# Operand sums moved to VectorE in halves, score masks moved to ScalarE and GpSimd: one fused retention and gated-unit kernel

## The chip, the cores and the metric

The kernel runs on one core of a Trainium2 chip. TensorE does the matrix products into PSUM; VectorE (DVE in the profile) and ScalarE (ACT) can read PSUM and SBUF; GpSimd (POOL) works here on SBUF only; SyncE (SP) issues most of the transfers. Each engine runs its own queue in order and waits for the others by semaphores. The metric is the device time of one execution in microseconds (us), lower is better.

## The reference, cut to what matters

```python
scores = (1/sqrt(64)) * q @ k.T                     # batch 8, heads 8, sequence 576, head dim 64
Dmat   = where(i >= j, gamma_h ** (i - j), 0)       # causal, one decay per head
x      = (scores * Dmat) @ v                        # -> 4608 tokens x 512
h      = x @ w_in                                   # 512 -> 2048
out    = (h * cos(h)) @ w_out                       # 2048 -> 512
```

The decay is a product of a power for the row and one for the column, so the kernel folds it into q and k; of `Dmat` only the 0/1 causal mask is left to be applied to the scores. Only scores inside a group of 128 tokens are formed; what earlier tokens contribute comes through a carried state per head.

## The kernel before, in words

The 4608 tokens are 36 groups of 128 (`g`). Nine groups hold two sequences of 576; the fifth of the nine (`g % PER == MIX`: groups 4, 13, 22, 31) holds the end of one sequence and the start of the next, so its mask also cuts off one more 64x64 corner per head (`tri_mix`).

Work on a group, in this order:

- `load`: three transfers (`fq`, `fk`, `fv`) on SP's queue, in rings of five buffers.
- `prep` (lines 140 and 156): GpSimd multiplies q and k by their powers into `qks` and casts v into `vb`; beyond group 25 ScalarE does the cast. `transposes` then puts a transposing transfer on SP's queue.
- `scores` (lines 195 and 207): TensorE writes the 8 heads' 128x128 scores of a group into one PSUM tile (tag "a" or "b"), VectorE multiplies them by the mask into `ret` (bf16, in SBUF; four buffers).
- `states`: TensorE forms k·v of a group, VectorE adds it to the running state (`s32`, lines 285 and 287), ScalarE casts it.
- `attn_out` (lines 319 and 333): for a pair of groups, TensorE multiplies `ret` by v (`own`, line 333) and then the carried state by q (line 319); ScalarE evacuates the result as `xT` (line 350).

The dense part goes in ten tiles of tokens, `widths = [512, 256, 256] + [512] * 7`. `mm1` (line 365) makes eight blocks of h per 512 tokens, each a PSUM tile of 128x1024 from the three tags a, b and m in turn; ScalarE computes the cosine (`cosh`, line 373), VectorE the product `gT` (line 374). A block can only start when the `gT` of the block three before it has read its PSUM tile.

Tiles n = 0, 1, 2 multiply `gT` by `w_out` directly (`mm2`). From n = 3 (`S7`) on, `mm2_seven` does the second product as a 2x2 block product in seven products instead of eight. `gT` is split in two halves r of the tokens and two halves k of the 2048 features. Each of the seven products is 16 matmuls of 256 columns (line 517) over eight features blocks. They run in the order 3, 4, 5, 2, 1, 7, 6. Products 3 and 4 take quarters of `gT` as they are; the others take a sum or difference of two quarters, a tile `gs` of 8 x 256 per partition:

```python
5: ((0, 0), (0, 1), ALU.add),      # (r, k) of the first quarter, of the second, operation
2: ((1, 0), (1, 1), ALU.add),
1: ((0, 0), (1, 1), ALU.add),
7: ((0, 1), (1, 1), ALU.subtract),
6: ((1, 0), (0, 0), ALU.subtract),
```

`g_sum` (line 445) makes them: the fifth, and a few others in tiles 3 and 9, on VectorE in pieces of 128x1024 or more, all the rest on GpSimd in pieces of 128x512, four for one sum. A hand-made dependency ("port free") holds the first GpSimd piece after a VectorE piece until that one is done. Results are combined in SBUF tiles `ot` (lines 537 and 559 on VectorE, 557, 564 and 569 on ScalarE) and stored.

Between the seven products the attention of the next tile's groups is placed (`at`, with `unit7`): two units in a tile, each with `states`, `attn_out` of one pair and `scores2` of the next pair. For n = 5 and later these stand ahead of product 4 and ahead of product 1. In tiles 3 and 4 `scores2` alone stands ahead of product 5, and units stand ahead of products 1 and 6. The order on every engine is the program's order (`manual_schedule`); nothing reorders it. After each of the four stores of a tile `feed` appends the next `prep`, transposes and loads: none after the first store, one group after the second, one after the third and two after the fourth.

Of the kernel before, what the change touches and what calls it, by code (L numbers as in the profile page):

```python
# [13 lines left out]
ALU = mybir.AluOpType  # L14
# [3 lines left out]
def kernel(  # L18
# [16 lines left out]
    nc = tc.nc  # L35
    P = 128
    B, H, S, D = q.shape
# [7 lines left out]
    PER = 2 * S // P  # L45
    MIX = PER // 2
    HP = P // 2
# [8 lines left out]
    N_PE_T = 6  # L56
    S7 = 3
    LD = 5

    consts = ctx.enter_context(tc.tile_pool(name="consts", bufs=1))  # L60
    first = ctx.enter_context(tc.tile_pool(name="first", bufs=1))
# [38 lines left out]
    tiles = {}  # L100
# [86 lines left out]
    def scores(g, bank, idle=0, parts=1, put_off=None):  # L187
        qks, vb, qkT, qT = tiles["a", g]
        ps = psum.tile([P, 2, HG, P], F32, tag=bank, name="sc")
        warm(ps[:, 0].rearrange("p b i -> p (b i)"), idle)  # L190
        for hg in range(HG):
            for i0 in range(0, P, P // parts):
                for he in range(2):
                    d0, i1 = he * D, i0 + P // parts
                    nc.tensor.matmul(  # L195
                        ps[i0:i1, he, hg, :],
                        lhsT=qkT[d0 : d0 + D, HG + hg, i0:i1],
                        rhs=qT[d0 : d0 + D, hg, :],
                        start=True,
                        stop=True,  # L200
                    )
        ret = retp.tile([P, 2, HG, P], BF16, tag="ret", name="ret")
        mask = tri_mix if g % PER == MIX else tri
        tiles["ret", g] = ret

        def masked():
            nc.vector.tensor_tensor(  # L207
                out=ret.rearrange("p a b i -> p (a b) i"),
                in0=ps.rearrange("p a b i -> p (a b) i"),
                in1=mask.unsqueeze(1).to_broadcast([P, H, P]),  # L210
                op=ALU.mult,
            )

        if put_off is None:
            masked()
        else:
            put_off.append(masked)
# [207 lines left out]
    def g_sum(n, x, e0, e1):  # L425

        gT = tiles["g", n]
        a, b, op_ = {
            5: ((0, 0), (0, 1), ALU.add),
# [4 lines that stand above are left out]
        }[x]  # L434
        if ("gs", n, x) not in tiles:
            tiles["gs", n, x] = sump.tile([P, E2, 256], BF16, tag=f"gs{x}", name=f"gs{x}")
        on_dve = x == 5 or (n, x) == (S7, 2) or (n, x, e0) in (
            (S7, 1, 4), (last, 1, 0), (last, 2, 4)
        )
        step = e1 - e0 if on_dve else 2  # L440
        for e in range(e0, e1, step):
            i0, i1 = (
                gT[:, k * E2 + e : k * E2 + e + step, r * 256 : (r + 1) * 256] for r, k in (a, b)
            )
            i = (nc.vector if on_dve else nc.gpsimd).tensor_tensor(  # L445
                out=tiles["gs", n, x][:, e : e + step], in0=i0, in1=i1, op=op_
            )
            if on_dve:
                tiles["gate"] = i
            elif "gate" in tiles:  # L450
                tc.add_manual_dep(
                    i.ins,
                    tiles.pop("gate").ins.name,
                    mybir.DependencyInfo(mybir.DependencyClass.Sync, mybir.DependencyReason.DATA),
                    reason="port free",
                )

    def sums_after(n, i):

        if n == S7:  # L460
            if i < 4:
                w_sums(3 + i % 2, i // 2 * 4, i // 2 * 4 + 4)
            elif i < 6:
                g_sum(n, 5, i % 4 * 4, i % 4 * 4 + 4)
                if i == 5:
                    g_sum(n, 6, 0, 4)
            elif i == 7:
                g_sum(n, 2, 0, E2)
                g_sum(n, 1, 4, E2)
                g_sum(n, 1, 0, 4)  # L470
                for e in (0, 4):
                    g_sum(n, 7, e, e + 4)
                prep_next(kv_first=True)
                g_sum(n, 6, 4, E2)
        elif n == S7 + 1 and i in (3, 7):
            for x in (5, 2, 1):
                g_sum(n, x, i - 3, i + 1)
            for x in (7, 6) if i == 7 else ():
                for e in (0, 4):
                    g_sum(n, x, e, e + 4)  # L480
        elif i == 3:
            for x in (5, 2, 1, 7, 6) if n < last else (5, 1, 2, 7, 6):
                g_sum(n, x, 0, 4)
        elif i == 7 and n == last:
            late_sums(n)

    def late_sums(n):
        for x in (5, 2, 1, 7, 6):
            g_sum(n, x, 4, E2)

    def product(n, x):

# [34 lines left out]
    def mm2_seven(n, at):  # L527
# [4 lines left out]
        def flush():  # L532
            while pend:
                pend.pop(0)()
# [14 lines left out]
        for x in (3, 4, 5, 2, 1, 7, 6):  # L549
            if x in at:  # L550
                at[x](flush, pend)
            else:
                flush()
            parts = product(n, x)
            if x == 3:
                u22 = new("a")
# [37 lines left out]
    def prep_next(**kw):  # L594
        nonlocal prepared
        prep(prepared, **kw)
        prepared += 1
# [182 lines left out]
    for n, w in enumerate(widths):  # L780
# [28 lines left out]
        if n == 0:  # L809
            todo = [  # L810
                (34 + 5 * i, lambda x=x, e=e: w_sums(x, e, e + 4))
                for i, (x, e) in enumerate((x, e) for x in (1, 6, 7) for e in (0, 4))
            ] + [
                (45, lambda: transposes(4, "ab")),
                (49, lambda: state(4)),
                (50, lambda: scores(4, "a")),
                (57, lambda: attn_out([4], "a")),
                (61, lambda: transposes(5, "ba")),
                (63, lambda: state(5)),
            ]  # L820
        elif n == 1:
            todo = pair(6, "ab", 16, 27)
        elif n == 2:
            todo = [(11, lambda: scores2(g)), (25, lambda: unit(g, "m", soon=True))]
            late += [lambda: unit(g + 2, "b", False)]
        else:
            at = {}
            if n + 1 < len(widths):
                at = {
                    4: lambda then, off: unit7(g, "st", True, lambda: late_sums(n), off),  # L830
                    1: lambda then, off: unit7(g + 2, "n", True, then),
                }
                if n in (3, 4):
                    at = {
                        5: lambda then, off: (then(), scores2(g)),
                        1: lambda then, off: unit7(g, "n", True, then),
                        6: lambda then, off: unit7(g + 2, "b", n > 3, then),
                    }
            mm2_seven(n, at)
            continue  # L840
# [43 lines left out]
```

## Time and profile before

| What | Value |
|---|---|
| Device time, three runs | 301.53 us median (300.94 to 304.33) |
| Profiled execution, first to last instruction | 298.2 us |
| TensorE | 287.1 us busy, 3113 matmuls |
| VectorE | 207.9 us busy, 245 instructions |
| ScalarE | 135.9 us busy, 167 instructions |
| GpSimd | 209.4 us busy, 214 instructions |
| `gs` sums on GpSimd, 128x512 | 102, together 116.3 us |
| `gs` sums on VectorE | 18, together 20.4 us |
| score masks on VectorE, 128x1024 | 36, together 43.0 us |
| `gT` on VectorE, 128x1024 | 72, together 87.8 us |
| Granted TensorE clock | 1.000 of full speed |

The profile gives the span of one execution; around it lie the 3.3 us by which the median of the runs is longer. Busy time counts from an instruction's start to its end, waits for a port of the memory inside it included; a time in brackets behind an instruction is idle time before it, with what ended it. Start times are from the beginning of the span. Tile 3's `mm1` starts at 84.18 us, those of tiles 4 to 9 at 116.78, 149.83, 179.84, 209.19, 238.62 and 267.81.

### The profile page before, as it was taken

Reading aid. Unit: us, or ns where it says so; the run is one execution under the profiler, and the core shown is the slowest. Engines: PE = TensorE matmul, PEld = TensorE weight load, DVE = VectorE, ACT = ScalarE, POOL = GpSimd, SP = SyncE. Lnnn points to the kernel's source line nnn. Section 1 sums busy time; section 2 is a strip of 40 time slices with the busy share of each in tenths; the row PEclk is TensorE's granted clock in tenths of the full one; section 3 lists DMA queues with packets and bytes.
Section 4 is the critical chain, followed back from the end, with each engine's and each line's share of the span. In section 5 each row is a group of like instructions: output and inputs, shape, how many; then the busy total and the mean of one; then the engine's idle time right before and its main releaser. Section 6 shows DMA issues by size and latency. Waiting matters only on the chain.

```text
span 298.2 us, 7384 instructions
## 1 busy us (share of the span) xinstructions
PE 287.1 (96%) x3113; PEld 195.3 (65%) x3113; DVE 207.9 (70%) x245; ACT 135.9 (46%) x167; POOL 209.4 (70%) x214
## 2 busy tenths in 40 slices
PE   8899999999999999979999999999999999999995
PEld 3478646848578786448744875488448845874584
DVE  5677637564579994788848874887489757935872
ACT  2656433514255432642346554546464446425620
POOL 2750066436445599997999999599959946980693
PEclk9999999999999999999999999999999999999999
DMA  7999999999999999999999997998690260031013
GB/s 203 212 209 206 209 214 213 200 243 208 208 174 222 211 239 213 217 279 176 198 224 229 209 200 183 212 208 201 122 194 2 73 143 0 2 106 36 0 44 99
DMA packets 154304, 50.28 MB, mean 169 GB/s; under 512 B 140832, under 2 KB 153248, under 8 KB 154272
## 3 DMA queue, kind: packets, MB, share of 16 engines
q1 hardware_dynamic: 149504, 45.10, 77.2%
q0 software_dynamic: 4224, 4.19, 8.5%
q8 instruction: 24, 0.39, 0.6%
q10 hardware_dynamic: 544, 0.52, 0.5%
q14 instruction: 8, 0.07, 0.1%
HBM read 36.70 MB, written 9.44 MB: 155 GB/s over the span
## 4 chain that ended last, share of the span: by engine, by line
PE 43%; POOL 25%; SPq 13%; DMA 8%; DVE 5%; issue 3%; ACT 1%; POOLq 0%; DVEq 0%
PE h L365 22%; POOL gs L445 17%; PE o L517 11%; SPq L117 8%; POOL qks L140 6%; PE o L382 5%; SPq L167 4%; DVE gT L374 3%; DMA fk<-in_k_dram 2%; DMA w_in_sb<-in_moe_w_in_dram 2%; DMA qkT<-qks 2%; POOL vb L156 2%; DVE gs L445 2%; DMA fv<-in_v_dram 1%; ACT cosh L373 1%
## 5 line engine op out<-in xcount | busy, mean ns | idle before, releaser
L445 POOL TENSOR_TENSOR gs<-gT 128x512 bf16<-128x512 bf16 x102 | 116.3, 1180 | 29.4 <-DVE gs L445 29.4
L365 PE MATMUL h<-xT,w_in_sb 128*128 128x512 bf16 (+2 forms) x832 | 127.6, 313 | 2.6 <-DVE gT L374 1.8
L374 DVE TENSOR_TENSOR gT<-h,cosh 128x1024 bf16<-128x1024 f32 x72 | 87.8, 1223 | 43.7 <-ACT cosh L373 40.7
L373 ACT ACTIVATE cosh<-h,half_pi 128x1024 f32<-128x1024 f32 x72 | 80.2, 1114 | 72.2 <-PE h L365 69.8
L365 PEld LDWEIGHTS <-w_in_sb 128*128 128x128 bf16 x832 | 75.9, 98 | 51.6 <-issue 3.0
L140 POOL TENSOR_TENSOR qks<-fq,gq 128x512 bf16<-128x512 f32 x32 | 34.0, 1062 | 40.9 <-DMA fq<-in_q_dram 40.9
L517 PEld LDWEIGHTS <-gs 128*128 128x128 bf16 x576 | 53.6, 98 | 10.1 <-POOL gs L445 2.9
L140 POOL TENSOR_TENSOR qks<-fk,gk 128x512 bf16<-128x512 f32 x35 | 37.3, 1066 | 8.0 <-DMA fk<-in_k_dram 7.4
L207 DVE TENSOR_TENSOR ret<-sc,tri 128x1024 bf16<-128x1024 f32 x32 | 38.1, 1217 | 2.8 <-PE sc L195 2.7
L517 PE MATMUL o<-ws,gs 128*128 128x256 bf16 (+1 forms) x352 | 39.1, 268 | 0.7 <-POOL gs L445 0.5
L382 PE MATMUL o<-w_out_sb,gT 128*128 128x512 bf16 x128 | 30.1, 380 | 0.0
L517 PE MATMUL o<-w_out_sb,gT 128*128 128x256 bf16 x224 | 26.6, 273 | 0.1
L517 PE MATMUL o<-w_out_sb,gs 128*128 128x256 bf16 x224 | 26.1, 273 | 0.5 <-POOL gs L445 0.4
L537 DVE TENSOR_TENSOR ot<-o,ot 128x512 f32<-128x512 f32 (+2 forms) x25 | 14.9, 603 | 14.7 <-PE o L517 14.5
L517 PEld LDWEIGHTS <-gT 128*128 128x128 bf16 x224 | 21.4, 98 | 4.7 <-DVE gT L374 0.7
L350 ACT CAST xT<-ov 128x1024 bf16<-128x1024 f32 (+1 forms) x18 | 16.5, 917 | 16.1 <-PE ov L319 13.9
L445 DVE TENSOR_TENSOR gs<-gT 128x1024 bf16<-128x1024 bf16 (+1 forms) x18 | 20.4, 1148 | 0.3
L382 PEld LDWEIGHTS <-gT 128*128 128x128 bf16 x128 | 11.8, 98 | 12.5
L156 POOL CAST vb<-fv 128x512 bf16<-128x512 f32 x22 | 14.3, 651 | 4.4 <-DMA fv<-in_v_dram 4.2
L564 ACT COPY ot<-o 128x512 f32<-128x512 f32 x7 | 4.1, 586 | 20.5 <-PE o L517 20.5
L392 ACT COPY ot<-o 128x512 f32<-128x512 f32 x8 | 4.7, 588 | 17.4 <-PE o L382 17.4
L537 DVE TENSOR_TENSOR ot<-ot,o 128x512 f32<-128x512 f32 x14 | 9.6, 684 | 4.0 <-ACT ot L569 2.4
(70 smaller groups left out, 175.8 us busy)
## 6 DMA issues: line engine op xcount, KB each, us to landing
out_dram<-ot SPq DMA_DIRECT2D x35, 256.0 KB, 4.0
fk<-in_k_dram SPq DMA_DIRECT2D x32, 256.0 KB, 5.2
fv<-in_v_dram SPq DMA_DIRECT2D x32, 256.0 KB, 5.2
fq<-in_q_dram SPq DMA_DIRECT2D x30, 256.0 KB, 4.5
w_in_sb<-in_moe_w_in_dram POOLq DMA_DIRECT2D x4, 512.0 KB, 8.9
w_out_sb<-in_moe_w_out_dram POOLq DMA_DIRECT2D x4, 512.0 KB, 16.2
fq<-in_q_dram SPq DMA_DIRECT2D x8, 128.0 KB, 4.0
fk<-in_k_dram SPq DMA_DIRECT2D x8, 128.0 KB, 4.4
```

The lines of the kernel that those rows point to most:

```text
L117: i = nc.sync.dma_start(f[p0:p1], src[b, :, s0 : s0 + p1 - p0, :].rearrange("h s d -> s h d"))
L140: eng.tensor_tensor(out=qks[:, m].rearrange("p (b a) d -> p a b d", a=2), in0=f.rearrange("p (a b) d -> p a b d", a=2), in1=by[:, c, :].re ...
L156: copy_v(vb, fv)
L207: nc.vector.tensor_tensor(out=ret.rearrange("p a b i -> p (a b) i"), in0=ps.rearrange("p a b i -> p (a b) i"), in1=mask.unsqueeze(1).to_br ...
L350: evac(tiles["x", n][:, :, t0 : t0 + len(gs) * P], ps.rearrange("p c x i -> p c (x i)"))
L365: nc.tensor.matmul(ps[:, j, :], lhsT=w_in_sb[:, dg, (et + j) * P : (et + j + 1) * P], rhs=xT[:, dg, c0 : c0 + w], start=(dg == 0), stop=(d ...
L373: nc.scalar.activation(cosh, ps, ACTF.Sin, bias=half_pi, scale=1.0)
L374: nc.vector.tensor_mul(gT[:, et : et + m, c0 : c0 + w], ps, cosh)
L382: nc.tensor.matmul(ps, lhsT=gT[:, et, tsi * P : (tsi + 1) * P], rhs=w_out_sb[:, et, :], start=(et == 0), stop=(et == ET - 1),)
L445: i = (nc.vector if on_dve else nc.gpsimd).tensor_tensor(out=tiles["gs", n, x][:, e : e + step], in0=i0, in1=i1, op=op_)
L517: nc.tensor.matmul(dst[i], lhsT=lhs[:, e, j * P : (j + 1) * P], rhs=rhs[:, e, c0:c1], start=(x in (3, 4, 1, 7) and e == 0 and (i == 0 or l ...
L537: pend.append(lambda: nc.vector.tensor_tensor(out=out_, in0=in0, in1=in1, op=op_))
```

## The change

All `gs` sums of tiles 3 to 9 go to VectorE, in halves of 128x1024 (ten for one tile, 70 in all), and the hand-made dependency goes. Their places in VectorE's queue are new: `sums_after` puts the first halves of sums 5, 2 and 1 behind `mm1` blocks 3, 4 and 5, `sums_before` puts the others ahead of the products, behind what `flush` or the unit has queued. In tile 3 the places differ: sums 5 and the first half of 6 within `mm1`, the second half of 6 ahead of product 4, sums 2, 1 and 7 ahead of products 5, 2 and 1.

From group 16 (`SEL`) on, 20 groups in all, the mask on VectorE is replaced by two steps: ScalarE copies the scores from PSUM into `ret`, and GpSimd sets the masked part of `ret` to zero in place (for groups 22 and 31 with a further `memset` of the corner). The copies stand in ScalarE's queue behind the `xT` evacuation of their unit and ahead of the casts of the state. `put_off` has no effect there any more.

The program order of TensorE and the order of SP's transfers are the same in both kernels.

```diff
+    SEL = 16
...
-        if put_off is None:
+        if g >= SEL:
+            nc.scalar.copy(ret.rearrange("p a b i -> p (a b) i"), ps.rearrange("p a b i -> p (a b) i"))
+            ret8 = ret.rearrange("p a b i -> p (a b) i")
+            nc.gpsimd.affine_select(
+                ret8, ret8, pattern=[[0, H], [1, P]], compare_op=ALU.is_ge, fill=0.0, base=0,
+                channel_multiplier=-1,
+            )
+            if g % PER == MIX:
+                nc.gpsimd.memset(ret8[:HP, :, HP:], 0.0)
+        elif put_off is None:
             masked()
...
-        on_dve = x == 5 or (n, x) == (S7, 2) or (n, x, e0) in (
-            (S7, 1, 4), (last, 1, 0), (last, 2, 4)
-        )
-        step = e1 - e0 if on_dve else 2
-        for e in range(e0, e1, step):
...
-            i = (nc.vector if on_dve else nc.gpsimd).tensor_tensor(
-                out=tiles["gs", n, x][:, e : e + step], in0=i0, in1=i1, op=op_
-            )
...
+        nc.vector.tensor_tensor(out=tiles["gs", n, x][:, e0:e1], in0=i0, in1=i1, op=op_)
+
+    def g_halves(n, *which):
+
+        for x, half in which:
+            g_sum(n, x, 4 * half, 4 * half + 4)
 
     def sums_after(n, i):
 
         if n == S7:
             if i < 4:
                 w_sums(3 + i % 2, i // 2 * 4, i // 2 * 4 + 4)
...
+            g_halves(n, *{4: [(5, 0)], 5: [(5, 1)], 6: [(6, 0)]}.get(i, ()))
+        else:
+            g_halves(n, *{3: [(5, 0)], 4: [(2, 0)], 5: [(1, 0)]}.get(i, ()))
+
+    def sums_before(n, x):
+
+        if n == S7:
+            todo = {4: [(6, 1)], 5: [(2, 0), (2, 1)], 2: [(1, 0), (1, 1)], 1: [(7, 0), (7, 1)]}
+        else:
+            todo = {5: [(1, 1)], 2: [(7, 0), (7, 1)], 1: [(6, 0), (6, 1)]}
+            if n < last and n != S7 + 1:
+                todo[5].insert(0, (2, 1))
+            else:
+                todo[4] = [(5, 1), (2, 1)]
+        g_halves(n, *todo.get(x, ()))
...
                 at[x](flush, pend)
             else:
                 flush()
+            sums_before(n, x)
             parts = product(n, x)
...
-                    4: lambda then, off: unit7(g, "st", True, lambda: late_sums(n), off),
+                    4: lambda then, off: unit7(g, "st", True, lambda: g_halves(n, (5, 1)), off),
```

## The prediction

> **What bounds the kernel now.** The page comes first: TensorE is busy 96% of the span and its granted clock is full in all 40 slices.
>
> ```profile
> PE 287.1 (96%) x3113; PEld 195.3 (65%) x3113; DVE 207.9 (70%) x245; ACT 135.9 (46%) x167; POOL 209.4 (70%) x214
> PEclk9999999999999999999999999999999999999999
> ```
>
> Second, the list of waits for TensorE alone: all that an easier GpSimd or VectorE could give back stands here.
>
> ```profile
> PE h L365 <- DVE gT L374: 1.8, 1, 1.8
> ...
> PE o L517 <- POOL gs L445: 0.9, 3, 0.4
> ```
>
> With the gaps that the timeline shows ahead of matmuls, from tile 3 on I count 0.45 (108.28 us), 1.78 (130.81), 0.46 (147.28), 0.27 (149.38), 0.40 (172.48), 0.23 (267.36) and about 0.40 near 293.4: 4.0 us. That is the ceiling of the gain. The chain of waits puts 17% of the span on POOL gs L445, but most of that time TensorE was busy beside it.
>
> Third, the timelines of VectorE and GpSimd around the largest gap.
>
> ```profile
> 125.03 1.23 DVE L374 TENSOR_TENSOR gT<-h,cosh 128x1024 bf16<-128x1024 f32 x1 [0.50 <-ACT cosh L373]
> 126.30 3.33 DVE L445 TENSOR_TENSOR gs<-gT 128x1024 bf16<-128x1024 bf16 x1
> 126.48 1.03 POOL L140 TENSOR_TENSOR qks<-fq,gq 128x512 bf16<-128x512 f32 x1
> 127.48 1.03 POOL L140 TENSOR_TENSOR qks<-fk,gk 128x512 bf16<-128x512 f32 x1
> 128.47 0.60 POOL L156 CAST vb<-fv 128x512 bf16<-128x512 f32 x1
> 130.81 1.89 PE L365 MATMUL h<-xT,w_in_sb 128*128 128x512 bf16 x8 [1.78 <-DVE gT L374]
> ```
>
> A sum on VectorE that takes 0.69 alone (135.14 and 189.35 us, GpSimd idle) took 3.33 here: it ended 0.56 after GpSimd's run ended. Now a case inside a run of GpSimd:
>
> ```profile
> 226.28 1.67 DVE L445 TENSOR_TENSOR gs<-gT 128x1024 bf16<-128x1024 bf16 x1
> 226.25 1.16 POOL L445 TENSOR_TENSOR gs<-gT 128x512 bf16<-128x512 bf16 x1
> 227.36 1.62 POOL L445 TENSOR_TENSOR gs<-gT 128x512 bf16<-128x512 bf16 x1
> ```
>
> Here it waited for the one operation that was running (to 227.41), and the next one was stretched by 0.46. So a sum on VectorE costs what is left of GpSimd's operation plus 0.6, and pushes GpSimd by up to 0.6. Operations with one operand in PSUM (gT, masks, combinations) keep their 1.23, 1.21 and 0.69 beside a busy GpSimd. Of the contended sums one (126.30) lost to several operations, the others (159.35, 166.92, 196.47, 226.28, 255.72, 284.23) to one.
>
> **The change part by part.** TensorE's and SP's orders stay the same, so time can only come from waits.
>
> Busy sums. VectorE loses 20 masks of 1.21 (24 us) and 18 sums (20.4 us) and gets 70 halves; at 0.6 from start to start these are 42 us, about even. GpSimd loses 116 us and gets 20 selects and 2 memsets. ScalarE gets 20 copies of 128x1024; the same shape from PSUM takes 1.01 (xT L350), start to start 0.91: 18 us on an engine at 46%. No engine becomes full; what decides is who stands in front of whom.
>
> The select. Only a 128x128 shape is in the trace:
>
> ```profile
> 1.61 0.20 POOL L655 MEMSET tri<- 128x128 f32 x1
> 1.89 0.29 POOL L656 TENSOR_SCALAR_AFFINE_SELECT tri<-tri 128x128 f32<-128x128 f32 x1
> ```
>
> A memset of 128x1 takes 0.105. With that as fixed part the select costs (294 - 105)/127 = 1.49 ns per element, and 1024 elements 1.6 us. Low end: memset's (198 - 105)/127 = 0.73 ns, 0.85 us. High end: eight times 294 ns, 2.35 us. I take 1.6, worked out from the select's own row. The Trainium skill, "GPSIMD Engine Reference", section 4.1, says that one-input operations on GpSimd run at roughly line rate; at that page's 1.2 GHz my estimate would be 0.96 us for the select, near the low end, and the sum below would come out near 303.
>
> One tile, worked out on tile 6 (start 179.84), in page times. TensorE's side:
>
> ```profile
> 196.43 0.62 PE L195 MATMUL sc<-qkT 64*64 64x128 bf16 x32
> 196.98 1.92 PE L517 MATMUL o<-w_out_sb,gT 128*128 128x256 bf16 x16
> 198.74 3.77 PE L517 MATMUL o<-w_out_sb,gs 128*128 128x256 bf16 x32
> 203.39 0.62 PE L195 MATMUL sc<-qkT 64*64 64x128 bf16 x32
> 203.94 5.42 PE L517 MATMUL o<-ws,gs 128*128 128x256 bf16 x48
> ```
>
> That is: scores, product 4, products 5 and 2, scores, products 1, 7 and 6 (1.75 each, so 6 starts at 207.44 and its second half at 208.3).
> - ScalarE: xT ends at 197.67, then the copies end at 198.58 and 199.50.
> - GpSimd: first select 198.6 to 200.2. VectorE wants the second half of sum 2 at 199.45, behind the combination that waits for product 4; it gets 200.2 to 200.8 (wanted by product 2 at 201.4: in time). Second select to 202.4, wanted by attn_out at 203.0: in time. Second half of sum 1 to 203.0, combination to 203.6.
> - The next prep (two operations of 1.0) and the two halves of sum 7 now take turns: 203.0 to 204.0 and 204.6 to 205.6 for GpSimd, 204.0 to 204.6 and 205.6 to 206.2 for VectorE; product 7 wants them at 205.7 and 206.6: in time.
> - VectorE: two state additions and a combination to 207.7. The second pair of copies is ready at 205.5 and 206.45, so its selects start at 206.2. Sum 6 takes turns with them: select to 207.8, first half to 208.4, select to 210.0, second half to 210.6. TensorE wanted them at 207.44 and, once late, at 209.28: stalls of 0.96 and 1.32, **2.3 us**.
>
> The same steps give 0.1 with a select of 0.85, and 5.3 with 2.35 (0.2 on sum 2, 0.7 in attn_out, 4.4 on sum 6). Within mm1 the added half sums (gT's spacing leaves 0.49 idle between two) delay gT by 0.1 to 0.3 against a margin of 0.76 to the block that needs its PSUM: nothing, as long as GpSimd is idle there; by the same walk its preps end about 6 us into mm1, the first sum comes at 9.6. If that cover goes, a case like 126.30 comes back, 1.78 each.
>
> Tiles 5, 6, 7: 3 x 2.3, less the 0.40 in tile 5: +6.5.
>
> Tile 4 has scores three times, two of them only two products ahead of their use. GpSimd between the first two pairs: selects from 137.6 (3.2), the prep of group 22 with its casts (1.0 + 1.0 + 0.6 + 0.6), four sums let in between (2.4), so 146.4; the next selects end at 148.0 and 149.6. TensorE wants them at 145.75 and 0.3 after it starts: 2.25 + 1.3 = 3.5. Against this, the 1.78 goes, because VectorE's first sum then meets no prep (they have ended before), and the 0.27 behind POOL gs: +1.5. With the low end 0.55 - 2.05 = -1.5, with the high end +4.5. Group 22's casts also wait for a transfer that landed only around 152 in the trace; the selects are queued behind them. I take it as landed, since SP's queue is held by preps that come no later than now.
>
> Tile 3 has no selects, but its masks are still on VectorE, and the sums 2 and 7 stand behind them. VectorE: gT ends 0.6 later, at 103.2 (half of sum 6 is ahead of it); other half 103.8; combination, after product 4 (104.1), 104.8; two masks 107.1; sum 2 at 107.7. Product 2 was due at 106.45: 1.25, less the 0.45 that now stands behind it. Then combination, sum 1 (110.15), state additions, combination (111.7), two masks (114.0), sum 7 at 114.6, where product 7 is due at 112.85: 1.75. By the end of product 7, 116.35 against 113.45: +2.9. GpSimd's preps of groups 16 to 18 run here as their loads land; I add one 0.6 for a sum that meets one: +3.5.
>
> Tiles 8 and 9: one pair of selects or none, so the sums are early; the 0.23 and 0.40 go: -0.6.
>
> **Sum**: 3.5 + 1.5 + 6.5 - 0.6 = +10.9 us on a span of 298.2. The median of the runs (301.53) is 3.3 above that span, which I carry over: 312.4. With the low end 3.5 - 1.5 - 0.1 - 0.6 = +1.3, 302.8; with the high end 3.5 + 4.5 + 15.5 - 0.6 = +22.9, 324.4.
>
> **The rivals.**
> - *Cheap select*, up to about 1.1 us: the turns end in time, only tile 3 pays. 303 to 305. For it: 128 elements are few to split a fixed part from, and the cast in 0.60 for 512 elements is 1 ns per element. Chance 0.22.
> - *Starved sums*: what happened at 126.30 becomes the rule, since selects and preps now stand back to back. In tile 6 sum 2 would wait out both selects and the prep, to 204.4, and product 2 stalls by about 3.2; in three tiles and with tile 4 some 10 us on top, 322; a select near 2.35 leads there too. Against it: six of seven contended sums waited for one operation only. Chance 0.20. The Trainium skill, "SBUF — State Buffer", says of the shared port that whoever starts first holds it for the whole instruction and the other blocks; by that a wait is one operation long, and the row at 126.30, lost to two that started later, goes beyond it. By the rule alone the sum stays at mine.
> - *Faster*: the sums come out of GpSimd's queue and all 4.0 us of stalls go, 297.5. It needs a select under 0.9 us and tile 3's sums ready in time, that is VectorE some 1.5 us earlier behind the masks of tile 3; decided from 3 us of stalls removed and less than 1 added. Chance 0.08.
> - *The change does nothing*: excluded, the orders on three engines differ.
>
> **How the numbers follow.** The forecast, 312.4, has 0.50. A difference of 1% (3 us) is about what a measurement of this kernel can tell from no change. Faster by over 1% (below 298.5): 0.07. Within 1%: 0.15, most of the cheap select. Slower: 0.78. The range goes from the low end, 302.8, to the starved case, 322.
>
> **What would show it.** In tiles 5 to 7: gaps ahead of product 6, released by DVE gs, of 1 to 2.5 us; VectorE's sums at 1 to 2.3 us in the second half of a tile and at 0.69 in mm1; the select's duration itself. In tile 4: a gap in attn_out released by POOL. In tile 3: gaps ahead of products 2 and 7 released by DVE gs. The gap at 130.8 gone. I am wrong if the select is near 1 us, if sums beside it keep 0.69, or if preps wait for loads with selects behind them.

## The result and the profile after

| | before | after |
|---|---|---|
| Device time, median of four runs each | 301.39 us (300.94 to 304.33) | 312.62 us (308.91 to 314.47) |
| Ratio after to before, 95% interval | | 1.0355 [1.0273, 1.0437] |
| Span of the profiled execution | 298.2 us | 312.7 us (time 314.47) |
| Mean granted clock of TensorE in it | 1.000 | 0.989 |
| Sums `gs` on VectorE | 18, together 20.4 us | 70, together 63.0 us |
| VectorE / GpSimd busy | 207.9 / 209.4 us | 225.0 / 123.2 us |

The changed kernel is slower by 3.6%. Its four runs lie 1.8% apart, and they go with the clock: 308.91 us at a mean granted clock of 1.000, 312.39 at 0.995, 312.84 at 0.993 and 314.47 at 0.989. The profiled execution is the last of these; the record counts it as slow, so the ratio goes by the other three, and below tile 3 and the clock are read again in runs that are not slow.

The page of after, parts 1 and 2 (busy times; then 40 slices of the span, PEclk in tenths):

```profile
PE 288.8 (92%) x3091; PEld 197.5 (63%) x3113; DVE 225.0 (72%) x277; ACT 154.1 (49%) x187; POOL 123.2 (39%) x134
PEclk9999999999999978999999999999999999999999
```

TensorE went from 96% to 92%: it has the same work and waits more (of its 3113 matmuls this trace lacks 22 records). The two slices below 9 hold a second loss, a clock that was not granted in full around 110 to 125 us. The three largest waits of TensorE in after (total, times, longest):

```profile
PE o L504 <- DVE gs L450: 4.5, 3, 2.1
PE o L504 <- DVE s L297: 3.6, 3, 1.8
PE st L276 <- DVE ot L524: 2.2, 1, 2.2
```

Before, the longest wait was one `gT` of 1.8. Now VectorE ends nearly all of them, by sums (L450), but also by state additions (L297) and combinations (L524) that stand behind sums in its queue.

By tile, from the start of one `mm1` to the next (tile 9 to the last matmul), both profiled executions:

| Tile | before, us | after, us | difference | forecast |
|---|---|---|---|---|
| ahead of tile 3 | 84.18 | 86.32 | +2.1 | 0 |
| 3 | 32.60 | 40.81 | +8.2 | +3.5 |
| 4 | 33.05 | 31.98 | -1.1 | +1.5 |
| 5 | 30.01 | 32.11 | +2.1 | +1.9 |
| 6 | 29.35 | 31.30 | +1.95 | +2.3 |
| 7 | 29.43 | 31.49 | +2.1 | +2.3 |
| 8 and 9 | 56.02 | 55.02 | -1.0 | -0.6 |

The 2.1 us ahead of tile 3 are transfers (1.5 for a piece of `w_in`, 0.7 for a `qkT`) in code that the change doesn't touch; in the ten profiles of the experiments tile 3 starts at 83.9 to 85.0.

**Tiles 5 to 7.** Tile 6 shows the mechanism. The timeline of after, all three engines, second half of the tile:

```profile
210.04 2.58 POOL L218 TENSOR_SCALAR_AFFINE_SELECT ret<-ret 128x1024 bf16<-128x1024 bf16 x2 [14.32 <-ACT ret L216]
210.99 2.18 DVE L450 TENSOR_TENSOR gs<-gT 128x1024 bf16<-128x1024 bf16 x2
212.60 1.47 POOL L141 TENSOR_TENSOR qks<-fq,gq 128x512 bf16<-128x512 f32 x1
213.09 0.67 DVE L524 TENSOR_TENSOR ot<-ot,o 128x512 f32<-128x512 f32 x1
213.69 2.38 DVE L450 TENSOR_TENSOR gs<-gT 128x1024 bf16<-128x1024 bf16 x2
214.03 1.49 POOL L141 TENSOR_TENSOR qks<-fk,gk 128x512 bf16<-128x512 f32 x1
216.00 0.41 DVE L295 COPY s<-st 128x256 f32<-128x256 f32 x1
216.44 0.42 DVE L297 TENSOR_TENSOR s<-st,s 128x256 f32<-128x256 f32 x1
216.92 3.67 PE L504 MATMUL o<-ws,gs 128*128 128x256 bf16 x32 [1.53 <-DVE s L297]
```

Of the four sums from 210.99 on, three meet GpSimd and take 1.57, 0.93 and 1.53 in place of 0.68. Each waits for the operation that runs, then goes, and the next operation is stretched by up to 0.46 (a prep's 1.04 becomes 1.47 and 1.49). The additions L295 and L297 are queued behind them. They read the PSUM tile with tag `n`, and product 1 writes a tile of the same tag, so it waits: 1.53. The chain of after goes the same way; these are its longest pieces (start, duration):

```profile
208.95 1.03 ACT ret L216
211.12 2.05 DVE gs L450 x2
213.77 2.30 DVE gs L450 x2
217.46 2.67 DVE gs L450 x2
220.78 1.91 PE o L504 x16
```

**Tile 3.** The timeline of TensorE in after:

```profile
107.28 1.92 PE L504 MATMUL o<-w_out_sb,gs 128*128 128x256 bf16 x16
111.29 3.33 PE L504 MATMUL o<-w_out_sb,gs 128*128 128x256 bf16 x16 [2.09 <-DVE gs L450]
...
116.39 1.92 PE L504 MATMUL o<-ws,gs 128*128 128x256 bf16 x16
120.31 1.05 PE L504 MATMUL o<-ws,gs 128*128 128x256 bf16 x8 [2.00 <-DVE gs L450]
121.75 1.66 PE L504 MATMUL o<-ws,gs 128*128 128x256 bf16 x8 [0.40 <-DVE gs L450]
```

Products 2 and 7 wait for sums that stand behind the two masks, as the walk had it. VectorE's timeline of after, ahead of product 2:

```profile
108.61 1.22 DVE L208 TENSOR_TENSOR ret<-sc,tri_mix 128x1024 bf16<-128x1024 f32 x1
109.74 2.94 DVE L450 TENSOR_TENSOR gs<-gT 128x1024 bf16<-128x1024 bf16 x2
```

The pair of sums takes 2.94 beside preps (2.80 at 118.90), where a pair alone takes 1.28 (113.21). But look at TensorE's durations too: sixteen matmuls take 1.92 at 107.28 and 3.33 at 111.29. The windows view of after gives the clock beside it (stretch, its length, busy time and count of each engine, PEclk, DMA share, GB/s):

```profile
112.00:118.00 6.00, 6.00 (x107) 4.32 (x106) 5.21 (x9) 2.21 (x4) 4.24 (x5) 0.73 1.12 238
118.00:124.00 6.00, 3.60 (x41) 2.30 (x41) 4.85 (x5) 0.00 (x0) 3.79 (x4) 0.84 1.21 221
```

By the trace's record of the clock it stood at half speed from 111.79 and from 122.03, for 3.41 us each. Each of the two stretches does half its work and so costs, by an estimate, up to 1.7 us, together up to 3.4 of the 8.2. The rest, about 5, is stalls: 2.09, 2.00 and 0.40 here, and 0.38 and 0.69 within `mm1` and in product 4, behind `gT`, less the 0.45 of before.

Four runs below have the same program in tile 3 and the clock at full speed there in their profiles: tile 3 takes 36.03 us with another order of the later sums, 36.23 and 36.33 with two other ways to clear the corner, and 38.20 with the sums alone. So the stalls without the clock cost 3.4 to 5.6 us, and the 8.2 of the table is a bad case.

One part of the change that bears on tile 3 isn't in the diff above: before, `sums_after` calls `prep_next` behind the last block of tile 3's `mm1`, and the prep of group 16 runs behind six pieces of sums on GpSimd (at 111.46). After, that call is gone, and `feed` makes this prep behind the tile's first store. Preps then run from 106.08 on, beside the sums.

**Tile 4.** The gap of 1.78 ahead of `mm1`'s block is gone; 1.35 ahead of product 1 (behind a state copy on VectorE) came in.

### The profile page after: what moved, and what is told of

It is laid out like the page before. It is cut to its first block, busy times and chain, and to the rows that moved or that the text cites. A ratio compares the mean times of both kernels' runs of the same rounds, so it can differ in the third digit from the quotient of the medians.

```text
span 312.7 us, 7322 instructions
## 1 busy us (share of the span) xinstructions
PE 288.8 (92%) x3091; PEld 197.5 (63%) x3113; DVE 225.0 (72%) x277; ACT 154.1 (49%) x187; POOL 123.2 (39%) x134
## 4 chain that ended last, share of the span: by engine, by line
PE 39%; DVE 10%; SPq 8%; DMA 5%; issue 2%; ACT 1%; POOL 1%; DVEq 0%; ACTq 0%
PE h L375 21%; PE o L504 15%; DVE gs L450 6%; SPq L118 5%; DMA fq<-in_q_dram 5%; SPq L168 2%; DVE ot L524 1%; ACT ret L216 1%; DVE ot L547 1%; PE ov L343 1%; PE sc L196 1%; DVE ret L208 1%; POOL qks L141 1%; PE ov L329 1%; DVE s L297 1%
## 5 line engine op out<-in xcount | busy, mean ns | idle before, releaser
L450 DVE TENSOR_TENSOR gs<-gT 128x1024 bf16<-128x1024 bf16 x70 | 63.0, 923 | 0.3
L218 POOL TENSOR_SCALAR_AFFINE_SELECT ret<-ret 128x1024 bf16<-128x1024 bf16 x20 | 24.8, 1260 | 84.7 <-ACT ret L216 69.9
L141 POOL TENSOR_TENSOR qks<-fq,gq 128x512 bf16<-128x512 f32 x32 | 35.6, 1113 | 52.7 <-DMA fq<-in_q_dram 49.2
L141 POOL TENSOR_TENSOR qks<-fk,gk 128x512 bf16<-128x512 f32 x35 | 39.1, 1118 | 9.3 <-DMA fk<-in_k_dram 8.4
L392 PE MATMUL o<-w_out_sb,gT 128*128 128x512 bf16 x120 | 28.9, 380 | 0.5 <-issue 0.2
L504 PE MATMUL o<-w_out_sb,gs 128*128 128x256 bf16 x224 | 27.2, 280 | 2.1 <-DVE gs L450 2.1
L524 DVE TENSOR_TENSOR ot<-o,ot 128x512 f32<-128x512 f32 (+2 forms) x25 | 14.7, 602 | 14.1 <-PE o L504 13.8
L216 ACT CAST ret<-sc 128x1024 bf16<-128x1024 f32 x20 | 19.3, 1025 | 1.5 <-PE sc L196 1.5
L208 DVE TENSOR_TENSOR ret<-sc,tri 128x1024 bf16<-128x1024 f32 x14 | 16.7, 1220 | 2.8 <-PE sc L196 2.7
L402 ACT COPY ot<-o 128x512 f32<-128x512 f32 x8 | 4.7, 588 | 18.0 <-PE o L392 18.0
L343 PE MATMUL ov<-ret,vb 128*64 128x128 bf16 x288 | 12.3, 226 | 0.1
```

Source lines behind the costliest of these rows:

```text
L141: eng.tensor_tensor(out=qks[:, m].rearrange("p (b a) d -> p a b d", a=2), in0=f.rearrange("p (a b) d -> p a b d", a=2), in1=by[:, c, :].re ...
L208: nc.vector.tensor_tensor(out=ret.rearrange("p a b i -> p (a b) i"), in0=ps.rearrange("p a b i -> p (a b) i"), in1=mask.unsqueeze(1).to_br ...
L216: nc.scalar.copy(ret.rearrange("p a b i -> p (a b) i"), ps.rearrange("p a b i -> p (a b) i"))
L218: nc.gpsimd.affine_select(ret8, ret8, pattern=[[0, H], [1, P]], compare_op=ALU.is_ge, fill=0.0, base=0, channel_multiplier=-1,)
L392: nc.tensor.matmul(ps, lhsT=gT[:, et, tsi * P : (tsi + 1) * P], rhs=w_out_sb[:, et, :], start=(et == 0), stop=(et == ET - 1),)
L450: nc.vector.tensor_tensor(out=tiles["gs", n, x][:, e0:e1], in0=i0, in1=i1, op=op_)
```

## The experiments

Four questions: do the selects' turns with the sums (the port) make the loss in tiles 5 to 7, or the order of VectorE's queue? Is tile 3 a matter of its own? What did each half of the change do? Why do some sums take not 1.6 but 3.7 us, and why does the clock fall? Ratios go against the kernel before on the same chip, whose medians were 299.6 to 300.2 us.

### Tile 3's sums as before

```diff
-        nc.vector.tensor_tensor(out=tiles["gs", n, x][:, e0:e1], in0=i0, in1=i1, op=op_)
+        on_dve = n > S7 or x in (2, 5) or (x, e0) == (1, 4)
...
-            todo = {4: [(6, 1)], 5: [(2, 0), (2, 1)], 2: [(1, 0), (1, 1)], 1: [(7, 0), (7, 1)]}
+            todo = {}
```

> The changed kernel, with tile 3's sums made as before the change (GpSimd in pieces of 128x512, VectorE for sum 5, sum 2 and half of sum 1); tiles 4 to 9 as changed. In the changed kernel's profile tile 3 took 40.8 us (from the start of its mm1 to that of tile 4's) against 32.6 before. Gaps theory: only the gaps that VectorE's queue makes ahead of products 2 and 7 go, with the two in mm1 and product 4, together 5 us; tile 3 back to some 36, the run at about 307. Clock theory: the two gaps of 2 us also bring TensorE's granted clock down (0.73 to 0.88 between 112 and 130 us in that profile, worth 6 x 0.27 + 6 x 0.16 + 6 x 0.12 = 3.3 us); with the gaps gone the clock stays at 1.00, tile 3 is back at about 32.6 and the run at about 304. Either way the gap of 1.8 us in tile 4's mm1 may come back, because the preps run later again.

Measured: 308.13 us, ratio 1.0283 [1.0244, 1.0322]. Tile 3 takes 32.65 us, its stalls behind sums are gone but for 0.21, and the clock is full there, as the clock theory had it. (The edit also puts the prep of group 16 back where it was, so it doesn't tell the sums' places from the prep's.) But part of the gain is given back: the gap ahead of a block of `mm1` in tile 4 returns (1.76 at 130.82, tile 4 34.35), and tile 5 takes 33.23, since now the clock falls there, behind a gap of 2.18 that after has too. The windows of this run show gap and fall side by side:

```profile
173.00:176.40 3.40, 1.22 (x29) 0.98 (x29) 3.40 (x3) 1.10 (x2) 1.83 (x2) 1.00 1.34 220
176.40:179.80 3.40, 3.40 (x76) 2.69 (x69) 3.33 (x7) 1.99 (x3) 0.00 (x0) 0.50 1.19 267
```

Tile 3 is a loss of its own; tiles 6 and 7 don't know of it (31.30 and 31.48).

### Another order of the sums

```diff
-            todo = {5: [(1, 1)], 2: [(7, 0), (7, 1)], 1: [(6, 0), (6, 1)]}
+            todo = {5: [], 2: [(1, 1)], 1: [(7, 0), (7, 1), (6, 0), (6, 1)]}
```

> The changed kernel, with only the places of three pieces in VectorE's queue moved in tiles 4 to 9: the second half of sum 1 from ahead of product 5 to ahead of product 2 (behind the combination that waits for product 5), sum 7 from ahead of product 2 to ahead of product 1 (behind the state additions and the combination that waits for product 2). GpSimd's work is the same. In the changed kernel TensorE waits 1.35, 0.36, 1.53 and 1.76 us ahead of product 1 in tiles 4 to 7, and 2.18 us ahead of the state matmuls in tile 5, all of them released by state additions or a combination that read the PSUM tile with tag n and stand behind sums in VectorE's queue. Queue theory: these gaps go, tiles 5 to 7 fall from 32.1, 31.3 and 31.5 to about 29.6, tile 4 by 1.3: minus 6 to 7 us, about 306. Port theory: the sums still lose the same time to GpSimd's reads, so the gap only moves to product 7 or 6, and the time falls by less than 2 us.

Measured: 314.12 us, ratio 1.0476 [1.0430, 1.0523]: no gain, against the queue theory. The state additions come earlier, and the gap moves behind them: in tile 5 0.82 ahead of product 1 and 2.49 ahead of product 6, in tile 7 1.26, 0.45 and 2.45, with a fall of the clock (35.81). Of tiles 4 to 7 only tile 6 got better (30.14). VectorE's timeline in tile 7:

```profile
243.57 5.92 DVE L450 TENSOR_TENSOR gs<-gT 128x1024 bf16<-128x1024 bf16 x4
```

Four sums in a row take 5.92; alone, two pairs of 1.28 would be 2.6. In this order too the sums have to pass beside the operations of GpSimd; one other order doesn't show that no order helps, and tile 6 gained 1.2.

### No selects

```diff
-            nc.scalar.copy(ret.rearrange("p a b i -> p (a b) i"), ps.rearrange("p a b i -> p (a b) i"))
-            ret8 = ret.rearrange("p a b i -> p (a b) i")
-            nc.gpsimd.affine_select(
...
-                nc.gpsimd.memset(ret8[:HP, :, HP:], 0.0)
+            nc.scalar.activation(ret.rearrange("p a b i -> p (a b) i"), ps.rearrange("p a b i -> p (a b) i"), ACTF.Copy, bias=0.0, scale=0.0)
```

> The changed kernel without the selects on GpSimd; ScalarE's copy of the scores multiplies by zero in place of it, so the part of the attention inside a group is left out from group 16 on. Selects were 25 us of GpSimd's time, in front of which VectorE's sums waited in the second half of tiles 4 to 7. Port theory: with GpSimd idle there except for preps, which now run ahead as soon as their loads are in, the sums fall to 0.6 to 0.7 us each, the state additions come in time, and tiles 4 to 7 lose their gaps: minus 6 to 7 us, about 306. Queue theory in its pure form: the order of VectorE's queue is the same, so most of the gaps (1.4 to 2.2 us each) stay and the run is at 310 or more. Tile 3 keeps its 41 us in both.

Measured: 305.27 us, ratio 1.0182 [1.0116, 1.0249]. Tiles 5 to 7 take 30.89, 29.46 and 29.58: 1.2, 1.8 and 1.9 less than in after, and in tiles 6 and 7 within 0.2 of before. VectorE's timeline in tile 6, the same instructions as above:

```profile
205.91 1.60 DVE L443 TENSOR_TENSOR gs<-gT 128x1024 bf16<-128x1024 bf16 x2
...
208.22 1.29 DVE L443 TENSOR_TENSOR gs<-gT 128x1024 bf16<-128x1024 bf16 x2
209.42 0.42 DVE L288 COPY s<-st 128x256 f32<-128x256 f32 x1
209.87 0.42 DVE L290 TENSOR_TENSOR s<-st,s 128x256 f32<-128x256 f32 x1
```

The pairs take 1.60 and 1.29 in place of 2.18 and 2.38, the additions follow in time and product 1 doesn't wait. Shown: in tiles 6 and 7 taking the selects off GpSimd takes away the loss, through the sums on VectorE; in tile 5 0.9 is left. That counts two effects together, since without the selects the preps of tile 6 run at 204.18 and 205.32, ahead of most of these sums, and no longer at 212.60 and 214.03, behind the selects and beside them. What is left of the loss is mostly tile 3 (39.13, one fall of the clock in it).

### One half of the change at a time

All sums on VectorE, all masks too:

```diff
-    SEL = 16
+    SEL = 36
```

> The sums' half of the change alone: all sums on VectorE in halves, every mask on VectorE as before; GpSimd has preps only. Port theory: without selects the sums of tiles 4 to 7 meet a GpSimd operation less often, but VectorE has four masks of 1.15 us more in a tile, two of them ahead of sum 6: gaps of about 0.5 ahead of products 1 and 6, tiles 5 to 7 at about 30.3 in place of 31.3 to 32.1; tile 3 is unchanged at 36 to 41 (its clock decides). About 309. If instead the change's loss were in the select alone, tiles 5 to 7 would be back at 29.4 and the run near 306.

Measured: 312.37 us, ratio 1.0426 [1.0352, 1.0499]. That is above the 309 expected, and not to be told from after. Tiles 5, 6, 7: 32.82, 31.23, 31.37, about what after has (32.11, 31.30, 31.49) and not the 30.3 expected, and tile 4 is worse (34.24). The mask's place hardly matters for tiles 6 and 7: on GpSimd it stretches the sums by the port, on VectorE it stands in the queue with them (gaps of 0.43 ahead of product 1 and 0.99 ahead of product 6 in tile 6, the last behind two masks that take 2.35).

Masks on ScalarE and GpSimd, sums as before:

```diff
+    SEL = 16
...
+            nc.scalar.copy(ret.rearrange("p a b i -> p (a b) i"), ps.rearrange("p a b i -> p (a b) i"))
...
+            nc.gpsimd.affine_select(
```

> The masks' half of the change alone: sums as before (most on GpSimd), masks from group 16 on by ScalarE's copy and GpSimd's select. GpSimd's queue in tiles 5 to 7 has 16 sum pieces of 1.12 us ahead of the first pair of selects; in the trace of before they end at 179.1 in tile 5, where attn_out of that pair wants its scores at 173.3. Gaps of some 7 us in attn_out in each of the tiles 4 to 7: 325 to 335, and the granted clock falls behind them. The two halves of the change would then be worth having only together. If the run is below 310, the reading of GpSimd's queue is wrong.

Measured: 350.31 us, ratio 1.1717 [1.1664, 1.1771], the slowest of all, and above the 325 to 335 expected. TensorE's waits and then GpSimd's timeline in tile 4:

```profile
PE ov L343 <- POOL ret L218: 32.1, 8, 10.0
PE ov L343 <- POOL ret L223: 8.2, 2, 7.2
```

```profile
135.28 13.36 POOL L455 TENSOR_TENSOR gs<-gT 128x512 bf16<-128x512 bf16 x12 [0.63 <-DVE gs L455]
148.59 2.14 POOL L218 TENSOR_SCALAR_AFFINE_SELECT ret<-ret 128x1024 bf16<-128x1024 bf16 x2
```

The selects stand behind twelve sums of 1.1 us each in GpSimd's queue, and `attn_out` waits 10 us for them. So each half is slower by itself: the sums alone give the whole loss, and the selects are bearable only when the sums are off GpSimd. On top, the clock falls behind each of the five long gaps (mean 0.936).

### The selects from group 12 on

```diff
-    SEL = 16
+    SEL = 12
```

> The changed kernel with the mask moved off VectorE from group 12 on, so that no mask stands ahead of sums 2 and 7 in VectorE's queue in tile 3. Queue theory: the gaps of 2.09 us ahead of product 2 and 2.00 us ahead of product 7 shrink by the two masks each (2.3 us), tile 3 falls from 40.8 to about 37, and to about 33.5 if the clock then stays at full speed: 305 to 309. Port theory for tile 3: the sums meet the preps of groups 16 to 18, gaps of about 1 us stay in the middle of product 2 or 7. Against both: the selects of groups 14 and 15 stand on GpSimd behind the prep of group 16, which waits for its loads; if that load is late, a gap comes up in attn_out instead.

Measured: 321.33 us, ratio 1.0637 [1.0560, 1.0713], outside all that was expected. The gap ahead of product 2 in tile 3 did go, since the masks no longer stand ahead of sum 2, but one of 12.50 us came ahead of product 1. VectorE's and GpSimd's timeline:

```profile
107.72 13.74 DVE L450 TENSOR_TENSOR gs<-gT 128x1024 bf16<-128x1024 bf16 x2
108.07 0.52 POOL L223 MEMSET ret<- 64x512 bf16 x1
108.56 1.04 POOL L141 TENSOR_TENSOR qks<-fq,gq 128x512 bf16<-128x512 f32 x1
```

The second of these sums wants the port at 108.48, during the memset, and gets it at 120.9, when GpSimd has run out of work: fourteen operations that started later went ahead of it. The starved sum, a rival in the prediction, exists; the question is when.

### What starves a sum

In after the one starved sum of tile 5 also stands behind a memset of the corner (64 partitions). GpSimd's and VectorE's timeline of after:

```profile
179.00 4.32 DVE L450 TENSOR_TENSOR gs<-gT 128x1024 bf16<-128x1024 bf16 x2
179.21 0.52 POOL L223 MEMSET ret<- 64x512 bf16 x1
179.68 1.08 POOL L218 TENSOR_SCALAR_AFFINE_SELECT ret<-ret 128x1024 bf16<-128x1024 bf16 x1
180.74 1.04 POOL L141 TENSOR_TENSOR qks<-fq,gq 128x512 bf16<-128x512 f32 x1
181.74 1.03 POOL L141 TENSOR_TENSOR qks<-fk,gk 128x512 bf16<-128x512 f32 x1
```

The second sum takes 3.71, and the select and the preps keep their short times: it never got between them. Two experiments replace the memset, first by a select on the same 64 partitions, then by one over all 128.

```diff
-                nc.gpsimd.memset(ret8[:HP, :, HP:], 0.0)
+                corner = ret8[:HP, :, HP:]
+                nc.gpsimd.affine_select(
+                    corner, corner, pattern=[[0, H], [0, HP]], compare_op=ALU.is_ge, fill=0.0,
+                    base=-1, channel_multiplier=0,
+                )
```

> The changed kernel with one thing replaced in groups 22 and 31: the corner is cleared by a second select, which reads SBUF, in place of the memset, which only writes. In tile 5 of the changed kernel a sum that arrived while that memset ran was passed by three GpSimd operations and took 3.71 us (2.18 us gap ahead of the state matmuls), and in the variant with selects from group 12 on one took 12.98 us behind another memset. If the memset is what lets the following operations pass, these sums take 1.6 us at most, tile 5 falls from 32.1 to about 31 and tile 7 by some 0.3: minus 1 to 1.5 us. If not, the 3.7 us stay.

Measured: 310.25 us, ratio 1.0363 [1.0310, 1.0415], as after. The sum is starved again, for 4.20 us, and the gap in tile 5 is 2.67. So it isn't the memset as such.

```diff
-                nc.gpsimd.memset(ret8[:HP, :, HP:], 0.0)
+                corner = ret8[:, :, HP:]
+                nc.gpsimd.affine_select(
+                    corner, corner, pattern=[[0, H], [0, HP]], compare_op=ALU.is_ge, fill=0.0,
+                    base=-HP, channel_multiplier=1,
+                )
```

> The corner of the mixed groups is cleared by a select over all 128 partitions (128x512) in place of the memset over 64. Theory A: a sum on VectorE loses to every operation that GpSimd starts afterwards, without a pause, when an operation on 64 partitions stands in that run (13 of 13 such cases so far); behind operations on 128 partitions it waits for one only. Then the second half of sum 1 in tile 5 takes 1.2 to 1.7 us in place of 3.71, the gap of 2.18 ahead of the state matmuls goes or falls below 0.5, tile 5 takes 30.6 to 31.6 us in place of 32.1, and the sum that took 2.07 in tile 7 takes 1.5 or less. Theory B: it is the run of operations without a pause that matters, whatever their shape: the sum in tile 5 stays at 3.7 to 4.2, the gap at 2.2 and tile 5 at 32.1. In all: 1 to 2 us less than the changed kernel under A, the same under B.

The two timelines, first with 64 partitions, then with 128:

```profile
173.29 4.81 DVE L454 TENSOR_TENSOR gs<-gT 128x1024 bf16<-128x1024 bf16 x2
173.50 0.99 POOL L224 TENSOR_SCALAR_AFFINE_SELECT ret<-ret 64x512 bf16<-64x512 bf16 x1
174.45 1.09 POOL L218 TENSOR_SCALAR_AFFINE_SELECT ret<-ret 128x1024 bf16<-128x1024 bf16 x1
```

```profile
172.92 1.74 DVE L454 TENSOR_TENSOR gs<-gT 128x1024 bf16<-128x1024 bf16 x2
173.13 0.99 POOL L224 TENSOR_SCALAR_AFFINE_SELECT ret<-ret 128x512 bf16<-128x512 bf16 x1
174.08 1.53 POOL L218 TENSOR_SCALAR_AFFINE_SELECT ret<-ret 128x1024 bf16<-128x1024 bf16 x1
```

Same operation, same 0.99 us, same moment; over 64 partitions the sum behind it waits out everything that follows, over 128 it goes next (1.13 us) and the select behind it is stretched to 1.53. The gap of 2.18 ahead of the state matmuls is gone. Tile 5 is at 31.38, 0.7 below after: within theory A's bounds, but gaps of 1.18 ahead of product 1 and 0.55 ahead of product 6 took the place of 2.18 and 0.36. In tile 7 the sum of 2.07 takes 1.55, just above the bound; the gap ahead of product 1 grew from 1.76 to 2.08 and brought a fall of the clock (33.36). The time of the whole is 310.85 us, ratio 1.0350 [1.0279, 1.0422]: theory A holds for the sum, and its gain for the whole can't be seen.

### Matmuls in the gaps of tile 3

```diff
+            if n == S7 and x in (2, 7):
+                warm(psum.tile([P, 512], F32, tag="m", name="idle"), 8)
```

> The changed kernel with 16 matmuls on zeros (128x512, 0.22 us each) that compute nothing, eight ahead of product 2 and eight ahead of product 7 of tile 3, where TensorE has gaps of 2.09 and 2.00 us. They add no wait as long as the gaps are longer than 1.75 us. Clock theory: the half-speed stretches of 3.41 us behind these two gaps go, the clock of every run is 0.997 or more, and the time falls by up to 3.4 us in the runs that had them (four runs had clocks 0.989, 0.993, 0.995 and 1.000 with spans 312.7, 311.0, 310.6 and 307.1): about 309, with less spread. If the clock fell for another reason, clocks stay at 0.99 and the time does not fall.

Measured: 309.29 us, ratio 1.0333 [1.0273, 1.0393]: by the time not to be told from after. The mean granted clock is 0.999 or 1.000 in all four runs, where after had 0.989 to 1.000, and tile 3 takes 39.21: the clock no longer falls there, so it is idle time of TensorE that brings it down. But the sums come no earlier, and the 3.5 us of added matmuls stand in the gaps; where the clock held without them, tile 3 took 36.03 to 38.20.

### Two repairs in the kernel before

```diff
-        on_dve = x == 5 or (n, x) == (S7, 2) or (n, x, e0) in (
+        on_dve = x == 5 or n == last or (n, x) == (S7, 2) or (n, x, e0) in (
...
-            for x in (5, 2, 1):
+            if i == 7:
+                g_sum(n, 5, 0, 4)
+                g_sum(n, 5, 4, E2)
+            for x in (2, 1):
```

This is the kernel before with what tiles 4 and 9 showed: in tile 4 the first sum on VectorE stands behind the last block of `mm1`, and in tile 9, where VectorE has no masks and GpSimd no selects, all sums are on VectorE.

> The kernel before with two places changed: in tile 4 sum 5 stands on VectorE behind the last block of mm1 and no longer ahead of a gT while GpSimd prepares groups, and all sums of tile 9 are on VectorE, where GpSimd and VectorE have little else to do. Theory: the gap of 1.78 ahead of the block of mm1 in tile 4 goes and most of the 0.40 in tile 9: 1.5 to 2.2 us, 0.5% to 0.7% less than the kernel before. Rival: the sum that comes later meets the same run of GpSimd and delays product 5, and the gap only moves: within 0.2% of the kernel before.

Measured, twelve runs: 298.70 us (297.93 to 299.26) against 299.76 (298.10 to 300.90), ratio 0.9969 [0.9952, 0.9987]: 0.3% faster than before, about half of what was expected. Tile 9 is shorter by 0.6. In tile 4 the 1.78 is gone, TensorE's timeline has all 64 matmuls of 512 columns in one piece:

```profile
116.65 13.98 PE L365 MATMUL h<-xT,w_in_sb 128*128 128x512 bf16 x64
...
144.19 0.61 PE L521 MATMUL o<-ws,gs 128*128 128x256 bf16 x4 [0.50 <-POOL gs L445]
```

but the tile takes 32.44 and not 31.3: gaps of 0.32 behind a combination and 0.19 and 0.50 behind GpSimd's sums came in. The rival of that run, that the gap only moves, is true for two thirds of it.

## Why the prediction was right, and where it wasn't

The forecast was 312.4, the median is 312.62, and slower was the likeliest sign. The direction was right, and so was the reason given for it: sums on VectorE wait for GpSimd, and what is queued behind them comes late. That the number fits to 0.2 is luck: several terms were off and made up for one another. By its own signs the prediction named itself wrong "if the select is near 1 us", and it is 1.09. Of the other signs the gaps ahead of products 2 and 7 in tile 3, the slow sums in the second half of the tiles and the end of the gap at 130.8 came; the gaps of 1 to 2.5 ahead of product 6 and the gap in `attn_out` of tile 4 didn't.

- **The select.** Taken at 1.6 from the 128x128 row; bounds 0.85 and 2.35. It takes 1.09 alone, by the view of the groups of after (shortest, median, longest in ns; the longest are stretched by sums):

```profile
L218 POOL TENSOR_SCALAR_AFFINE_SELECT ret<-ret x20: 1085/1092/1542, 146.1 to 274.0; 128x1024 bf16<-128x1024 bf16 x20
```

  That is nearest to the estimate of 0.96 from the Trainium skill, "GPSIMD Engine Reference", section 4.1, so the rule that spoke against my value was nearer than my reading of the row. The split of 294 ns into a fixed part and 1.49 ns per element was the mistake: from 128 (f32) to 1024 elements (bf16) the measured slope is (1092 - 294)/896 = 0.89 ns. With 1.09 the prediction's own steps give some 303 to 305.
- **Tiles 5 to 7, +6.5 forecast, +6.1 measured.** The size is right, the place and two terms are not. The step that failed is "Sum 6 takes turns with them", with stalls ahead of product 6 (0.19 there in tile 6). They stand ahead of product 1 and, in tile 5, ahead of the state matmuls, because the step let product 1 go as soon as its operands were there. It also needs the PSUM tile that the state additions read, and those are queued behind sums 1 and 7. The missed wait made up for the select that was sized too high. That sums and GpSimd take turns is shown by the rows of tile 6, and what it costs by the run without selects (1.2 to 1.9 us back in each tile).
- **Tile 3, +3.5 forecast, +8.2 measured, +3.4 to +5.6 where the clock held.** Products 2 and 7 as the places were right; the sums there met preps, and the stalls come to 2.09 and 2.40 in place of 1.25 and 1.75. A wait ahead of product 1, for state additions, wasn't in the walk (0.80 and 0.81 in the two profiles of 36.33 and 36.23). The step "delay gT by 0.1 to 0.3 ... nothing" failed here by 0.38 and 0.69: product 4 reads the last `gT` itself. The clock, up to 3.4 us in the profiled run, was in no step.
- **Tile 4, +1.5 forecast, -1.1 measured.** That the 1.78 goes was right. The 3.5 in `attn_out` never came, as the selects were done early (the low end of the range said -1.5); 1.35 ahead of product 1 came in, by the wait that was missed in tiles 5 to 7.
- **Tiles 8 and 9, -0.6 forecast, -1.0 measured.** Right.
- **Cheap select**, the rival at 0.22, gave 303 to 305 for a select up to 1.1. Its condition held and its time didn't (308.91 to 314.47): the price of a contended sum is not the select alone but the next operation, stretched by up to 0.46, and what is queued behind.
- **Starved sums**, at 0.20: real, but for a sum behind an operation on 64 partitions, and so for two groups of the twenty. *Faster* failed on both its conditions, the select (1.09, not under 0.9) and tile 3.
- **Smaller slips.** The sum at 126.30 lost to three operations that started later, not two: 126.48, 127.48 and 128.47. The 0.40 near 293.4 is idle time of weight loads; the matmuls' record has 0.12 there. And the 3.3 us carried over from the span are more than a run adds to its own span: 1.8 in each of after's four runs.

Two parts of the profiled difference of 14.4 us are not stalls of this queue: the 2.1 us ahead of tile 3, in code that the change doesn't touch, and the up to 3.4 us of the clock, which follow the change's gaps but differ from run to run. Without them its stalls come to 14.4 - 2.1 - 3.4 = 8.9 us, below the 10.9 forecast; the one run at full clock, 308.91, is 7.5 us above the median before.

## What to carry to other kernels

When work goes from one of two engines that share a port to the other, count the meetings and not the busy time: here VectorE and GpSimd together had 69 us less to do, and most sums that met GpSimd still cost about twice their time and pushed the next operation. For each instruction that comes later in a queue, list all that is behind it, and ask of every matmul not only when its operands are ready but who still has to read the PSUM tile that it writes. A gap of 2 us in a TensorE that is otherwise full can cost up to 1.7 more by the clock, so here two short gaps in different windows were better than one long one.

## What the runs showed of the hardware

**The clock falls by windows.** In the clock records of the twelve traces every stretch at half speed within the dense part lasts 3.41 us or a multiple (6.83, 10.24), and all of one run start on one grid of 3.41. Laid over the gaps of TensorE, with windows that come after 80 us and were at full clock themselves: all 13 in which it idled 1.98 us or more were followed by half speed; of some 35 with 1.2 to 1.8 us one was (1.72). The same gap can fall into one window or across two, as that of tile 5: 2.18 in one window in the run with tile 3's old sums (half speed follows), 1.68 and 0.50 in after (none). By an estimate from the half speed, runs of one kernel can so differ by up to 1.7 us for each such window. That it is idle time is shown by the matmuls on zeros: with them all four runs kept 0.999 or 1.000. The Trainium skill, "TensorE: Matmul & The Clock Gate", section "What's actually happening", has the free-running window of 3413 ns, which the records show; it names one idle window as the condition for half speed, and there these runs differ: 2.0 us of idle time within one window was enough.

**A pause decides who gets the port, and 64 partitions.** Of the sums on VectorE that met GpSimd in a run of operations without a pause, in the ten traces ahead of the last two: 13 of 13 lost to every later operation when the run had one on 64 partitions ahead of or at the meeting; of some 110 without one, all but three waited for the one that ran, and no longer. Where GpSimd paused behind such an operation, as for 0.07 us behind a cast over 64 partitions at 152.37 in after, the sum went in that pause (0.84 in all). With the corner over 128 partitions all contended sums waited for one. The three exceptions, all at about 126 us and behind a cast over 128 partitions (3.33 in before), stay open, so the 64 partitions are not the only way to starve a sum. The Trainium skill, "SBUF — State Buffer", section "SBUF: two separate sides", has an exclusive lock that whoever starts first holds for one instruction. That fits those that waited for one; the starved sums, one of which waited 12.4 us while fourteen operations started, go beyond it, and why the number of partitions should matter no run here shows.
